# A planner that counts slack behind copies, sums and low parts, and a second phase with fewer low parts on VectorE

## The chip, the core and the metric

The kernel runs on one core of a Trainium2 chip. The metric is device time in microseconds of one execution. The time before is the median of three runs, 1119.76 us (1118.62 to 1120.52). Instructions run on five engines, each in its own program order: PE (TensorE, the matrix products; PEld is its weight load), DVE (VectorE), ACT (ScalarE), POOL (GpSimd) and SP (SyncE, which issues most DMAs). They wait for each other by semaphores alone. An instruction that waits holds up all that stands behind it on its engine.

## The reference

Block-causal attention over 8 x 8 heads of 576 x 64, and behind it a feed-forward layer on 4608 tokens:

```python
scores = scale * np.matmul(q, k.transpose(0, 1, 3, 2))
scores = np.where(block_i >= block_j, scores, -1000000000.0)
attn = softmax(scores)
x = np.matmul(attn, v)          # reshaped to 4608 x 512
h = x @ w_in                    # 512 -> 2048
g = np.maximum(h, 0.0) + alpha * np.minimum(h, 0.0)
out = g @ w_out                 # 2048 -> 512
```

## The kernel before

**Two phases.** The first runs the attention and, beside it, 6 of the 16 blocks of 128 hidden columns. The second, from about 625 us on, runs the other 10, as 5 pairs (`NG`), over 9 blocks of 512 tokens. It computes both layers by a scheme of seven block products instead of eight (Strassen's, in Winograd's form).

**Operands in two parts.** A product of the second phase takes both operands as a high part (rounded to the matmul's type by ACT, line 532) and a low part (the rest: operand minus high part, line 533, on DVE or POOL). Each block product is six matmuls of 128x256: high x high, low x high and high x low, in two halves. I call those six matmuls one product.

**First layer of a pair** (`pair1`, product at line 722). Its seven products are, with the names that the texts below use: A (11·11), B (12·21), C (s2·t2), D (s1·t1), E (s3·t3), F (22·t4), G (s4·22). A, C, E and F add up in one PSUM bank, x. A is written; ACT copies the bank out (`keep`, line 731, u1); C is added onto it; ACT copies it again (u2); E is added; ACT copies it a third time (u3); F is added. So C, E and F must each wait until the copy before them has read x. B goes to bank y, and DVE adds u1 to it (`onto`, line 735). D goes to bank z. DVE then adds z to u3 (line 753), and only then may G be added onto z: **E, copy, DVE sum, G** is the longest chain of a pair. Relu and slope (`act`: line 739 on ACT, line 740 on DVE) make of the banks five tiles c, 128x256.

**Second layer** (`chunk2`, product at line 780). Seven products k = 0 to 6, each over the 5 pairs g, so 35 products a block. Each takes one tile c or a sum of such tiles, split into Gh (ACT, 532) and Gl (533). The low part is on DVE where g is odd (or, in the last block, where g is not 0), else on POOL. Of the sums (`plus`, line 765), three for each g come before k = 2 (`second`: s3, c12 + c22, then c12 - c11, all on DVE) and one before k = 6 (on POOL). `finish` and `onto` (798, 793) add the bank to what the first phase left.

**Beside it**, the seven operands X of the next 512 tokens are made (`factors`): sums at line 549 on DVE, split at 532 and 533, 128x512, three low parts on DVE and four on POOL.

**What sets the order.** A block's first-layer products run beside the second-layer products of the block before. Their order is made by a planner (`Plan.schedule`) when the program is built: it simulates the engines with a modelled cost for each operation (`c_dve`, `c_act`, `c_pool`, `c_mm`, all but PE times `LONGER`) and a latency behind it (`LAT`), and starts whatever is ready with the smallest `prio`. In the second phase a pair's product has `prio` = turn + k (`starts1`), a product of the second layer turn + g (`starts2`), and its split comes `LEAD` = 6 earlier. The modelled times order the instructions and nothing else: on the chip each engine runs them in that order and waits where an input is late.

Of the kernel before, what the change touches and what calls it, by code (L numbers as in the profile page):

```python
# [9 lines left out]
F32 = mybir.dt.float32  # L10
# [19 lines left out]
CHA = 256  # L30
# [107 lines left out]
class Plan:  # L138


    def __init__(self):
        self.ops, self.writer, self.readers = [], {}, {}
        self.free, self.tiles, self.quota, self.last = {}, {}, {}, {}

    def room(self, kind, n, make):
# [6 lines left out]
            have.append(slot)  # L152
        self.quota[kind] = self.quota.get(kind, 0) + n

    def op(self, engine, cost, fn, r=(), w=(), prio=0.0, claim=(), then=None, ends=()):

        i = len(self.ops)
        prio += SHIFTS.get(round(prio, 4), 0.0)
        deps = {j for j, o in enumerate(self.ops) if any(b.kind in ends for b in o[4])} if ends else set()
        for k in r:  # L160
            if k in self.writer:
                deps.add(self.writer[k])
        for k in w:
            if k in self.writer:
                deps.add(self.writer[k])
            deps.update(self.readers.get(k, ()))
        for k in r:
            self.readers.setdefault(k, []).append(i)
        for k in w:
            self.writer[k] = i  # L170
            self.readers[k] = []
        bufs = dict.fromkeys(k[0] if isinstance(k, tuple) else k for k in (*r, *w, *claim))
        bufs = [b for b in bufs if isinstance(b, Buf)]
        for b in bufs:
            b.users += 1
            if b.users == 1 and b.turn:
                b.after = self.last.get(b.turn)
                self.last[b.turn] = b
        deps.discard(i)
        self.ops.append((engine, cost, fn, deps, bufs, prio, then))  # L180
        return i

    def schedule(self):
# [43 lines left out]
        while events:  # L227
# [13 lines left out]
            for engine, heap in ready.items():  # L241
# [135 lines left out]
def attn_ffn(ctx, tc, qT, kT, vT, w_in, w_out, alpha, out):  # L377
# [149 lines left out]
            out=mb(), in0=mb(), scalar=2.0 ** -20, in1=eb(), op0=ALU.mult, op1=ALU.mult), r=[eb], w=[mb], prio=prio)  # L527
        return mb, mb

    def split(src, hi, lo, n, r, hk, lk, claim, on, prio):  # L530

        op("ACT", c_act(n, True), lambda: nc.scalar.copy(out=hi(), in_=src()), r=r, w=[hk], claim=claim, prio=prio)  # L532
        op(on, c_pool(n) if on == "POOL" else c_dve(n), lambda: (nc.gpsimd if on == "POOL" else nc.vector).tensor_tensor(  # L533
            out=lo(), in0=src(), in1=hi().bitcast(F32), op=ALU.subtract), r=[*r, hk], w=[lk], claim=claim, prio=prio)

    wts = {}

# [8 lines left out]

    def add(e, n, to, a, b, f, prio, r=()):

        op(e, c_pool(n) if e == "POOL" else c_dve(n), lambda: (nc.gpsimd if e == "POOL" else nc.vector).tensor_tensor(  # L549
            out=to[1](), in0=a[1](), in1=b[1](), op=f), r=[a[0], b[0], *r], w=[to[0]], prio=prio)  # L550

    w1s = {}
# [156 lines left out]
    def pair1(f, X, turn):  # L709

        W = w1s[f]
        ps = [Buf("bank", "hp", "hp") for _ in range(3)]
        cs = [Buf("c") for _ in range(5)]

        def product(bank, a, x, k, first):
            at, B = W1AT[a], X[x]

            def mm():
                n = 0
                for i, j in ((0, 0), (1, 0), (0, 1)):  # L720
                    for c in range(2):
                        nc.tensor.matmul(bank()[:, :CHA], W()[:, i, 256 * at + P * c:256 * at + P * c + P], B()[:, j, CHA * c:CHA * c + CHA],  # L722
                                         start=(first and n == 0), stop=(n == 5), skip_group_check=True)
                        n += 1
            op("PE", 6 * c_mm(CHA), mm, claim=[W, *(cs if k == 0 else ())],
               r=[(("w1", f, at // 2 * 2), "h"), (("w1", f, at // 2 * 2), "l"), (B, "h"), (B, "l")], w=[bank], prio=turn + k)

        def keep(bank):

            u = Buf("g")  # L730
            op("ACT", c_act(CHA), lambda: nc.scalar.copy(out=u(), in_=bank()[:, :CHA]), r=[bank], w=[u], prio=FP)
            return u

        def onto(bank, u):
            op("DVE", c_dve(CHA), lambda: nc.vector.tensor_tensor(out=bank()[:, :CHA], in0=bank()[:, :CHA], in1=u(), op=ALU.add), r=[u], w=[bank], prio=FP)  # L735

        def act(f, src, v, c):
            g = Buf("g")
            op("ACT", c_act(CHA), lambda: nc.scalar.activation(out=g(), in_=v(), func=AF.Relu, scale=-1.0), r=[src], w=[g], prio=FP)
            op("DVE", c_dve(CHA) + 60, lambda: nc.vector.scalar_tensor_tensor(  # L740
                out=c(), in0=g(), scalar=oal[:, f:f + 1], in1=v(), op0=ALU.mult, op1=ALU.add), r=[src, g, "oal"], w=[c], prio=FP)
        x, y, z = ps
        product(x, "11", "11", 0, True)
        u1 = keep(x)
        product(y, "12", "21", 1, True)
        onto(y, u1)
        act(f, y, lambda: y()[:, :CHA], cs[0])
        product(x, "s2", "t2", 2, False)
        u2 = keep(x)
        product(z, "s1", "t1", 3, True)  # L750
        product(x, "s3", "t3", 4, False)
        u3 = keep(x)
        op("DVE", c_dve(CHA), lambda: nc.vector.tensor_tensor(out=u3(), in0=z()[:, :CHA], in1=u3(), op=ALU.add), r=[z], w=[u3], prio=FP)  # L753
        act(f + 1, u3, u3, cs[3])
        product(x, "22", "t4", 5, False)
        act(f + 1, x, lambda: x()[:, :CHA], cs[2])
        product(z, "s4", "22", 6, False)
        onto(z, u2)
        act(f, z, lambda: z()[:, :CHA], cs[1])
        return cs  # L760

    def chunk2(t0, cs, turn, last):

        def plus(to, a, b, f, on, prio):
            op(on, c_pool(CHA) if on == "POOL" else c_dve(CHA), lambda: (nc.gpsimd if on == "POOL" else nc.vector).tensor_tensor(  # L765
                out=to(), in0=a(), in1=b(), op=f), r=[a, b], w=[to], prio=prio)

        def product(k, bank, c, at, first):

            for g in range(NG):  # L770
# [1 line left out]
                gh, gl, W, v = Buf("Gh"), Buf("Gl"), Buf("w2"), c(g, t - LEAD)  # L772
                op("SP", 256, lambda g=g, W=W: nc.sync.dma_start(out=W().bitcast(F32), in_=wd[at, :, g]),
                   r=[("wd", 1, at, g, x) for x in range(2)], w=[W], prio=t - AHEAD2)
                split(v, gh, gl, CHA, [v], gh, gl, [], "DVE" if g % 2 or last and g else "POOL", t - LEAD)

                def mm(g=g, gh=gh, gl=gl, W=W):
                    for i in range(2):
# [34 lines left out]
        def second(g, prio):  # L813

            c11, c12, _, c22, s3 = cs[g]
            plus(s3, c11, c12, ALU.subtract, "DVE", prio)
            plus(c12, c12, c22, ALU.add, "DVE", prio)
            plus(c11, c12, c11, ALU.subtract, "DVE", prio)
            return c11
        x, y, z = (Buf("bank", "acc") for _ in range(3))  # L820
        o11, o12, o22, o21 = (quarter(i, j) for i, j in ((0, 0), (0, 1), (1, 1), (1, 0)))
# [9 lines left out]
        finish(o22, z, 1, 1)  # L831
        product(5, x, lambda g, prio: cs[g][3], 4, False)
        finish(o21, x, 1, 0)
        product(6, z, sums(2, 2, 0, ALU.subtract, "POOL"), 3, False)
        finish(o12, z, 0, 1, 2 if last else 1)

    def chunk_a(t0, parts=(0, 1)):
# [433 lines left out]
```

## Time and profile before

| | |
|---|---|
| time, median of 3 runs | 1119.76 us (1118.62 to 1120.52) |
| the profiled execution, its own time | 1117.95 us |
| its span, first to last instruction | 1115.8 us |
| granted TensorE clock | 0.998 |
| PE, DVE, ACT, POOL busy | 96%, 73%, 63%, 60% |
| first matmul of `pair1` | 625.3 us |
| last matmul of `chunk2` | 1112.0 us |
| PE's waits in the second phase, 625 us to the end | 27.2 us in 30 waits |

The span is that of the profiled execution; what lies around it, 2.1 us, is launch and end. PE is the engine to look at: its idle time is what can go without fewer or shorter matmuls. A group row of the profile reads: line, engine, operation, tiles out<-in, shape, count | busy us, mean ns of one | idle time just before, and who ended it. A row of the timeline reads: start us, duration us, engine, line, operation, tiles, count, and in brackets the idle time before it with its releaser.

### The profile page before, as it was taken

The numbers are of one execution on the slowest core, as the hardware profiler recorded it, in microseconds if no ns is written. First come the engines' busy times: TensorE is split into PE (matmuls) and PEld (weight loads), VectorE is DVE, ScalarE is ACT, GpSimd is POOL, SyncE is SP. The second block draws the span as 40 slices with busy tenths as digits, with TensorE's granted clock in tenths as the row PEclk, the third lists the DMA queues.
The fourth block names the chain that finished last, engine by engine and source line by source line (L and its number), as shares of the span: only waits on it lengthen the run. The fifth ranks groups of instructions, "written<-read, shape, count | busy, mean of one in ns | idle before, by whom it ended". The sixth has DMA issues, their size and how long they took to land.

```text
span 1115.8 us, 24537 instructions
## 1 busy us (share of the span) xinstructions
PE 1073.9 (96%) x8158; PEld 969.9 (87%) x8158; DVE 814.1 (73%) x1779; ACT 701.4 (63%) x1969; POOL 666.2 (60%) x837
## 2 busy tenths in 40 slices
PE   7999999999999999999999989999999999999998
PEld 4668888888888888898888889999989898989998
DVE  8886685676575745757558598879696969787776
ACT  7788877776666766758555564555455555545554
POOL 4767757667676666666489574636272736364522
PEclk9999999999999999999999999999999999999999
DMA  6687886876668795749044436767676868686875
GB/s 193 194 257 214 233 246 169 267 209 194 193 176 248 217 270 157 214 140 271 32 175 152 174 119 199 243 212 243 211 253 202 276 193 280 188 267 196 270 259 162
DMA packets 139486, 233.37 MB, mean 209 GB/s; under 512 B 14816, under 2 KB 51680, under 8 KB 139360
## 3 DMA queue, kind: packets, MB, share of 16 engines
q1 hardware_dynamic: 138928, 231.53, 68.0%
q8 instruction: 65, 1.06, 0.4%
q14 instruction: 61, 0.50, 0.1%
q10 hardware_dynamic: 432, 0.27, 0.1%
HBM read 150.22 MB, written 37.49 MB: 168 GB/s over the span
## 4 chain that ended last, share of the span: by engine, by line
PE 85%; DVE 9%; ACT 2%; issue 2%; DMA 1%; POOL 1%; DVEq 0%; ACTq 0%; POOLq 0%
PE bank L780 17%; PE bank L722 16%; PE bank L646 13%; PE bank L679 13%; PE bank L1120 8%; PE bank L979 6%; PE bank L1019 6%; PE bank L1049 2%; DVE X L533 2%; DVE c L765 2%; PE bank L1076 1%; DVE xt L549 1%; DVE bank L735 1%; PE bank L984 1%; DVE gl L533 1%
## 5 line engine op out<-in xcount | busy, mean ns | idle before, releaser
L722 PE MATMUL bank<-X,w 128*128 128x256 f32 x1890 | 251.7, 284 | 23.0 <-DVE g L753 13.0
L722 PEld LDWEIGHTS bank<-X,w 128*128 128x128 f32 x1890 | 235.2, 189 | 28.8 <-DVE g L753 15.2
L780 PE MATMUL bank<-w,gh 128*128 128x256 f32 x1260 | 228.9, 280 | 0.8 <-ACT gh L532 0.8
L1011 POOL TENSOR_SCALAR p<-p,ri 128x256 f32<-128x256 f32 (+3 forms) x256 | 141.3, 567 | 90.9 <-DVE ri L1009 42.5
L780 PEld LDWEIGHTS bank<-w,gh 128*128 128x128 f32 x1260 | 193.6, 189 | 1.0 <-ACT gh L532 1.0
L780 PE MATMUL bank<-w,gl 128*128 128x256 f32 x630 | 177.6, 282 | 3.5 <-DVE gl L533 3.5
L533 POOL TENSOR_TENSOR gl<-c,gh 128x256 fp32r<-128x256 f32 x112 | 95.2, 855 | 121.4 <-ACT gh L532 120.3
L1003 ACT ACTIVATE p<-bank,nm 128x256 f32<-128x256 f32 (+3 forms) x256 | 133.9, 532 | 28.2 <-DVE nm L1000 13.8
L679 PE MATMUL bank<-wa,gh 128*128 128x512 f32 x432 | 140.1, 405 | 0.0
L646 PE MATMUL bank<-xh,wa 128*128 128x256 f32 x864 | 128.0, 287 | 0.0
L780 PEld LDWEIGHTS bank<-w,gl 128*128 128x128 f32 x630 | 118.9, 189 | 4.7 <-DVE gl L533 4.7
L532 ACT CAST gh<-c 128x256 fp32r<-128x256 f32 x198 | 79.7, 407 | 62.6 <-PE bank L780 60.6
L646 PEld LDWEIGHTS bank<-xh,wa 128*128 128x128 f32 x864 | 113.6, 190 | 2.7 <-issue 0.9
L1019 PE MATMUL bank<-ident,p 128*128 128x128 f32 x640 | 100.2, 277 | 5.0 <-POOL p L1011 2.9
L666 POOL TENSOR_TENSOR gl<-g,gh 128x256 fp32r<-128x256 f32 x108 | 83.2, 773 | 32.4 <-ACT gh L663 26.7
L1000 DVE TENSOR_REDUCE nm<-bank 128x1 f32<-128x384 f32 (+3 forms) x144 | 80.4, 587 | 22.5 <-PE bank L979 18.8
L979 PE MATMUL bank<-K,Q 128*128 128x512 f32 (+1 forms) x448 | 94.5, 331 | 1.1 <-ACT pl L1063 0.9
L1120 PE MATMUL bank<-PTF,vraw 128*64 128x320 f32 (+3 forms) x768 | 94.1, 384 | 0.5 <-ACT PTF L1096 0.5
L1019 PEld LDWEIGHTS bank<-ident,p 128*128 128x128 f32 x640 | 76.0, 142 | 16.8 <-POOL p L1011 6.6
L659 DVE SCALAR_TENSOR_TENSOR g<-g,oal,bank 128x256 f32<-128x256 f32 x108 | 51.4, 476 | 48.3 <-ACT g L657 47.9
L679 PEld LDWEIGHTS bank<-wa,gh 128*128 128x128 f32 x432 | 75.6, 189 | 12.4 <-issue 0.5
L679 PE MATMUL bank<-wa,gl 128*128 128x512 f32 x216 | 85.8, 397 | 0.1
(162 smaller groups left out, 2210.4 us busy)
## 6 DMA issues: line engine op xcount, KB each, us to landing
w<-wd SPq DMA_DIRECT2D x315, 256.0 KB, 4.0
Q<-QH SPq DMA_DIRECT2D x56, 256.0 KB, 3.9
K<-KH SPq DMA_DIRECT2D x112, 128.0 KB, 3.8
vraw<-in_v SPq DMA_DIRECT2D x32, 320.0 KB, 3.7
qraw<-in_q SPq DMA_DIRECT2D x30, 320.0 KB, 4.0
xd<-xT SPq DMA_DIRECT2D x8, 1152.0 KB, 6.5
part<-o SPq DMA_DIRECT2D x36, 256.0 KB, 3.5
xb<-xd SPq DMA_DIRECT2D x9, 1024.0 KB, 7.9
```

What stands on the lines that cost most here:

```text
L533: op(on, c_pool(n) if on == "POOL" else c_dve(n), lambda: (nc.gpsimd if on == "POOL" else nc.vector).tensor_tensor(out=lo(), in0=src(), in ...
L646: nc.tensor.matmul(hp()[:, :n], ww()[:, 0, cc * P:(cc + 1) * P], x()[:, cc, :n], start=(i == 0 and cc == 0), stop=(i == 2 and cc == NCC - 1))
L666: op("POOL", c_pool(CHA), lambda: nc.gpsimd.tensor_tensor(out=gl(), in0=g(), in1=gh().bitcast(F32), op=ALU.subtract), r=[g, gh], w=[gl], p ...
L679: nc.tensor.matmul(acc(), a()[:, ts], ww(), start=(first and i == 0), stop=(last and i == 2))
L722: nc.tensor.matmul(bank()[:, :CHA], W()[:, i, 256 * at + P * c:256 * at + P * c + P], B()[:, j, CHA * c:CHA * c + CHA], start=(first and n ...
L780: nc.tensor.matmul(bank()[:, CHA * i:CHA * i + CHA], a()[:, P * i:P * i + P], W()[:, x], start=(first and g + i + n == 0), stop=(g == NG - ...
L979: nc.tensor.matmul(o, Q()[:, i, qs], K()[:, 2 * h + i, :w], start=(i == 0), stop=(i == 1))
L1000: op("DVE", c_dve(w), lambda h=h: nc.vector.tensor_reduce(out=nm()[:, h:h + 1], in_=sb[h]()[:, off[h]:off[h] + w], axis=AX.X, op=ALU.max, ...
L1003: op("ACT", 238 + w / 1.2, lambda h=h, t=t: nc.scalar.activation(out=t()[:, :w], in_=sb[h]()[:, off[h]:off[h] + w], func=AF.Exp, bias=nm() ...
L1011: op("POOL", 244 + w / 1.2, lambda h=h: nc.gpsimd.tensor_scalar(out=pts[h]()[:, :w], in0=pts[h]()[:, :w], scalar1=ri()[:, h:h + 1], scalar ...
L1019: nc.tensor.transpose(out=tp()[:, base + c * P:base + (c + 1) * P], in_=pts[h]()[:, c * P:(c + 1) * P], identity=ident)
L1120: nc.tensor.matmul(ob()[rows[h], a - q0:q1 - q0], V()[:, c, h, :], moving, start=(c == 0), stop=(c == cs[-1][0]))
```

## The change

Four edits, all of them on the second phase:

- `SLACK`: 300 ns are added to the modelled latency behind `keep`'s copies, the sum of line 753 and the low parts of `chunk2`. `c_ss` (65 + 1.5 n ns) replaces `c_dve` (65 + n/0.96) as the modelled cost of DVE sums and low parts that read two tiles of SBUF. Both act on the planner alone.
- `LO_DVE = (1,)`: of the low parts of a block only that of g = 1 stays on DVE, and that of g = 3 goes to POOL (the last block keeps g = 1 to 4 on DVE).
- `SUMS`: of the three sums before k = 2, c12 + c22 and c12 - c11 go from DVE to POOL, and the sum before k = 6 goes from POOL to DVE.
- F and G get turn + 6 and + 7 instead of + 5 and + 6.

```diff
+SSN, SLACK = 1.5, 300
+SUMS, LO_DVE = ("DVE", "POOL", "POOL", "DVE"), (1,)
...
-                lat = LAT.get(engine, 0)
+                lat = LAT.get(engine, 0) + self.slack[chosen]
...
+def c_ss(n):
+    return SS(65 + n * SSN)
...
-    def split(src, hi, lo, n, r, hk, lk, claim, on, prio):
+    def split(src, hi, lo, n, r, hk, lk, claim, on, prio, slack=0):
...
-        op(on, c_pool(n) if on == "POOL" else c_dve(n), lambda: (nc.gpsimd if on == "POOL" else nc.vector).tensor_tensor(
-            out=lo(), in0=src(), in1=hi().bitcast(F32), op=ALU.subtract), r=[*r, hk], w=[lk], claim=claim, prio=prio)
+        op(on, c_pool(n) if on == "POOL" else c_ss(n), lambda: (nc.gpsimd if on == "POOL" else nc.vector).tensor_tensor(
+            out=lo(), in0=src(), in1=hi().bitcast(F32), op=ALU.subtract), r=[*r, hk], w=[lk], claim=claim, prio=prio, slack=slack)
...
-            op("ACT", c_act(CHA), lambda: nc.scalar.copy(out=u(), in_=bank()[:, :CHA]), r=[bank], w=[u], prio=FP)
+            op("ACT", c_act(CHA), lambda: nc.scalar.copy(out=u(), in_=bank()[:, :CHA]), r=[bank], w=[u], prio=FP, slack=SLACK)
...
-        product(x, "22", "t4", 5, False)
+        product(x, "22", "t4", 6, False)
         act(f + 1, x, lambda: x()[:, :CHA], cs[2])
-        product(z, "s4", "22", 6, False)
+        product(z, "s4", "22", 7, False)
...
-                split(v, gh, gl, CHA, [v], gh, gl, [], "DVE" if g % 2 or last and g else "POOL", t - LEAD)
+                split(v, gh, gl, CHA, [v], gh, gl, [], "DVE" if g in LO_DVE or last and g else "POOL", t - LEAD, SLACK)
...
-            plus(s3, c11, c12, ALU.subtract, "DVE", prio)
-            plus(c12, c12, c22, ALU.add, "DVE", prio)
-            plus(c11, c12, c11, ALU.subtract, "DVE", prio)
+            plus(s3, c11, c12, ALU.subtract, SUMS[0], prio)
+            plus(c12, c12, c22, ALU.add, SUMS[1], prio)
+            plus(c11, c12, c11, ALU.subtract, SUMS[2], prio)
...
-        product(6, z, sums(2, 2, 0, ALU.subtract, "POOL"), 3, False)
+        product(6, z, sums(2, 2, 0, ALU.subtract, SUMS[3]), 3, False)
```

`c_ss` also replaces `c_dve` in `add` and `plus`. The changed file has 11 lines more ahead of these places: 532, 533, 549, 722, 731, 735, 740, 753, 765 and 780 before are 543, 544, 560, 733, 742, 746, 751, 764, 776 and 791 after. The texts below use the numbers of before throughout.

Three places where the order changes:

**PE, the fourth pair of the 512 tokens 1536 to 2047.** Line 722 is a product of the pair, line 780 one of the second layer, four rows for its six matmuls. Before, from E (X0) over one product of the second layer to F (X6) and G (X1):

```order
L722 MATMUL bank1_180<-X0_6724,w14_7275 128x256 x6
L780 MATMUL bank4_207<-w25_7245,gh5_1120 128x256 x2
L780 MATMUL bank4_207<-w25_7245,gl5_1138 128x256
L780 MATMUL bank4_207<-w25_7245,gh5_1120 128x256 x2
L780 MATMUL bank4_207<-w25_7245,gl5_1138 128x256
L722 MATMUL bank1_180<-X6_7252,w14_7275 128x256 x6
L722 MATMUL bank0_178<-X1_6733,w14_7275 128x256 x6
```

Now, from E (X1) to F (X6) and G (X2):

```order
L733 MATMUL bank7_145<-X1_6732,w14_7277 128x256 x6
L791 MATMUL bank1_180<-w27_7252,gh1_610 128x256 x2
L791 MATMUL bank1_180<-w27_7252,gl1_631 128x256
L791 MATMUL bank1_180<-w27_7252,gh1_610 128x256 x2
L791 MATMUL bank1_180<-w27_7252,gl1_631 128x256
L791 MATMUL bank1_180<-w28_7257,gh2_680 128x256 x2
L791 MATMUL bank1_180<-w28_7257,gl2_698 128x256
L791 MATMUL bank1_180<-w28_7257,gh2_680 128x256 x2
L791 MATMUL bank1_180<-w28_7257,gl2_698 128x256
L733 MATMUL bank7_145<-X6_7254,w14_7277 128x256 x6
L733 MATMUL bank3_186<-X2_6753,w14_7277 128x256 x6
```

Two products instead of one now stand between E and F. In every pair but a block's first, D also goes ahead of C now, which puts two products (B and D) between A and C instead of one. Over a steady block, with "." for a product of the second layer and a bar behind each k, the PE order from k = 0 on was `.....|ABCD.E.FG...|.....|ABCD.E.FG...|ABCD.E.FG...|ABCDE.FG....|ABCD.E..FG..|`, and is now `G....A.|BCD.E..F.G.|.....|ABDC..E..FG.|ABDC..E..FG.|ABDC..E..FG.|ABDC..E..F.|`; the last G of a block now stands behind the bar.

**DVE, the fifth pair of the same tokens**, from `onto` (735) to the sum of line 753 that G waits for. Before:

```order
L735 TENSOR_TENSOR bank6_223<-bank6_223,g6_6804 128x256
L765 TENSOR_TENSOR raw1_176<-c10_7431,raw1_176 128x256
L533 TENSOR_TENSOR X5_7247<-xt1_6726,X5_7247 128x512
L740 SCALAR_TENSOR_TENSOR c17_7546<-g0_481,oal_83,bank6_223 128x256
L549 TENSOR_TENSOR xt1_6726<-xb0_6610,xt1_6726 128x512
L533 TENSOR_TENSOR X4_7241<-xt0_6712,X4_7241 128x512
L753 TENSOR_TENSOR g4_6761<-bank7_145,g4_6761 128x256
```

Now (735 is 746, 765 is 776, 533 is 544, 753 is 764):

```order
L746 TENSOR_TENSOR bank4_207<-bank4_207,g6_6792 128x256
L544 TENSOR_TENSOR X5_7250<-xt1_6734,X5_7250 128x512
L751 SCALAR_TENSOR_TENSOR c17_7543<-g5_6774,oal_83,bank4_207 128x256
L560 TENSOR_TENSOR xt1_6734<-xb0_6610,xt1_6734 128x512
L544 TENSOR_TENSOR X7_7471<-xt0_6712,X7_7471 128x512
L544 TENSOR_TENSOR gl4_951<-c2_7322,gh4_944 128x256
L764 TENSOR_TENSOR g0_481<-bank6_223,g0_481 128x256
```

The sum (765) has left this stretch and a low part (gl4) has come into it.

**POOL, from the middle of that pair to the first pair of the next tokens**, now:

```order
L776 TENSOR_TENSOR raw0_158<-raw0_158 128x256
L544 TENSOR_TENSOR X1_6732<-xb0_6610,X1_6732 128x512
L544 TENSOR_TENSOR gl5_1138<-c0_7226,gh5_1120 128x256
L544 TENSOR_TENSOR gl0_506<-raw1_176,gh0_495 128x256
L544 TENSOR_TENSOR X6_7254<-xt1_6734,X6_7254 128x512
L544 TENSOR_TENSOR gl1_631<-c17_7543,gh1_610 128x256
L544 TENSOR_TENSOR gl2_698<-c11_7507,gh2_680 128x256
L544 TENSOR_TENSOR gl4_951<-c6_7409,gh4_944 128x256
L544 TENSOR_TENSOR gl5_1138<-c8_7379,gh5_1120 128x256
L544 TENSOR_TENSOR gl0_506<-c4_7331,gh0_495 128x256
L544 TENSOR_TENSOR gl1_631<-raw1_176,gh1_610 128x256
L776 TENSOR_TENSOR c2_7322<-raw0_158,c2_7322 128x256
```

and ACT at the end of that stretch, where it rounds this c2 (543), between two copies of bank x of the next pair (742):

```order
L750 ACTIVATE g5_6774<-bank1_180 128x256
L742 COPY g0_481<-bank7_145 128x256
L543 CAST gh2_680<-c2_7322 128x256
L742 COPY g2_665<-bank7_145 128x256
L543 CAST gh3_824<-c0_7226 128x256
```

Ahead of these POOL rows stand X3, X0 and one more sum, behind them three more sums. The sum c2 was on DVE before; in its place POOL had sums for k = 6, whose results nothing needed soon. On ACT the copy u3 (g2, the second 742) stands behind the rounding of c2, as it did before.

More of the change, by code (lines that the diff above doesn't have):

```diff
@@ L141, in __init__ @@
     def __init__(self):
-        self.ops, self.writer, self.readers = [], {}, {}
+        self.ops, self.writer, self.readers, self.slack = [], {}, {}, []
         self.free, self.tiles, self.quota, self.last = {}, {}, {}, {}
@@ L153, in room, with op @@
         self.quota[kind] = self.quota.get(kind, 0) + n
-    def op(self, engine, cost, fn, r=(), w=(), prio=0.0, claim=(), then=None, ends=()):
+    def op(self, engine, cost, fn, r=(), w=(), prio=0.0, claim=(), then=None, ends=(), slack=0):
         i = len(self.ops)
@@ L180, in op @@
         self.ops.append((engine, cost, fn, deps, bufs, prio, then))
+        self.slack.append(slack)
         return i
@@ L321, in c_dve @@
     return 65 + n / 0.96
+class SS(float):
+    pass
+def c_ss(n):
+    return SS(65 + n * SSN)
 def c_dve2(n):
@@ L547, in add @@
     def add(e, n, to, a, b, f, prio, r=()):
-        op(e, c_pool(n) if e == "POOL" else c_dve(n), lambda: (nc.gpsimd if e == "POOL" else nc.vector).tensor_tensor(
+        op(e, c_pool(n) if e == "POOL" else c_ss(n), lambda: (nc.gpsimd if e == "POOL" else nc.vector).tensor_tensor(
             out=to[1](), in0=a[1](), in1=b[1](), op=f), r=[a[0], b[0], *r], w=[to[0]], prio=prio)
@@ L752, in pair1 @@
         u3 = keep(x)
-        op("DVE", c_dve(CHA), lambda: nc.vector.tensor_tensor(out=u3(), in0=z()[:, :CHA], in1=u3(), op=ALU.add), r=[z], w=[u3], prio=FP)
+        op("DVE", c_dve(CHA), lambda: nc.vector.tensor_tensor(out=u3(), in0=z()[:, :CHA], in1=u3(), op=ALU.add), r=[z], w=[u3], prio=FP, slack=SLACK)
         act(f + 1, u3, u3, cs[3])
-        product(x, "22", "t4", 5, False)
+        product(x, "22", "t4", 6, False)
         act(f + 1, x, lambda: x()[:, :CHA], cs[2])
-        product(z, "s4", "22", 6, False)
+        product(z, "s4", "22", 7, False)
         onto(z, u2)
@@ L764, in plus @@
         def plus(to, a, b, f, on, prio):
-            op(on, c_pool(CHA) if on == "POOL" else c_dve(CHA), lambda: (nc.gpsimd if on == "POOL" else nc.vector).tensor_tensor(
+            op(on, c_pool(CHA) if on == "POOL" else c_ss(CHA), lambda: (nc.gpsimd if on == "POOL" else nc.vector).tensor_tensor(
                 out=to(), in0=a(), in1=b(), op=f), r=[a, b], w=[to], prio=prio)
```

## The prediction

> **What bounds the kernel now.** The page first: PE is busy for nearly the whole span.
>
> ```profile
> PE 1073.9 (96%) x8158; PEld 969.9 (87%) x8158; DVE 814.1 (73%) x1779; ACT 701.4 (63%) x1969; POOL 666.2 (60%) x837
> ```
>
> The change leaves every matmul as it is, so it can win only idle time of PE. The view of waits of PE says where that lies. First 713.5 to 1034.8 us, six steady blocks of 53.55 us; then 625 to 713.5 (the run-in); then 1034.8 to the end.
>
> ```profile
> PE bank L722 <- DVE g L753: 7.7, 6, 1.3
> PE bank L722 <- ACT g L731: 5.0, 6, 0.9
> PE bank L780 <- DVE gl L533: 3.5, 6, 0.6
> ...
> PE bank L722 <- DVE g L753: 5.3, 5, 1.5
> PE bank L722 <- ACT g L731: 3.1, 4, 1.5
> PE bank L722 <- ACT X L532: 1.0, 1, 1.0
> ...
> PE bank L722 <- ACT g L731: 0.9, 1, 0.9
> PE bank L780 <- ACT gh L532: 0.8, 1, 0.8
> ```
>
> Each steady block has the same three waits, six times over: 1.28 us at G of its fifth pair, 0.83 at E of its first, 0.58 in a product of the second layer. The windows of one steady block and of the last block with pairs, which has one wait alone, bear that out:
>
> ```profile
> 767.10:820.70 53.60, 50.84 (x423) 50.18 (x422) 43.75 (x79) 28.94 (x77) 27.10 (x31) 1.00 0.73 231
> 1034.80:1086.00 51.20, 50.34 (x422) 50.10 (x421) 37.99 (x75) 26.61 (x72) 20.45 (x26) 1.00 0.83 273
> ```
>
> Columns are length, then busy us of PE, PEld, DVE, ACT, POOL. The timeline says why G waits:
>
> ```profile
> 812.39 0.43 DVE L735 TENSOR_TENSOR bank<-bank,g 128x256 f32<-128x256 f32 x1 [0.20 <-PE bank L722]
> 812.63 1.30 POOL L533 TENSOR_TENSOR X<-xb,X 128x512 fp32r<-128x512 f32 x1 [0.43 <-ACT X L532]
> 812.73 1.48 DVE L765 TENSOR_TENSOR raw<-c,raw 128x256 f32<-128x256 f32 x1
> 814.14 0.68 DVE L533 TENSOR_TENSOR X<-xt,X 128x512 fp32r<-128x512 f32 x1
> 814.33 0.88 PE L722 MATMUL bank<-X,w 128*128 128x256 f32 x6
> ...
> 815.04 0.40 PE L780 MATMUL bank<-w,gh 128*128 128x256 f32 x2
> 815.13 1.39 DVE L549 TENSOR_TENSOR xt<-xb,xt 128x512 f32<-128x512 f32 x1
> 816.21 1.45 POOL L533 TENSOR_TENSOR X<-xb,X 128x512 fp32r<-128x512 f32 x1 [0.24 <-ACT X L532]
> 816.44 1.77 DVE L533 TENSOR_TENSOR X<-xt,X 128x512 fp32r<-128x512 f32 x1
> 816.44 0.87 PE L722 MATMUL bank<-X,w 128*128 128x256 f32 x6
> 818.13 0.41 DVE L753 TENSOR_TENSOR g<-bank,g 128x256 f32<-128x256 f32 x1
> 818.60 0.97 PE L722 MATMUL bank<-X,w 128*128 128x256 f32 x6 [1.28 <-DVE g L753]
> ```
>
> DVE runs without a gap from line 735 to line 753, and the sum that G needs is last in its queue. A product takes 0.71 us (814.33 to 815.04). F to G took 2.16 instead, and G's own six matmuls 0.97 instead of 0.87: this wait costs 2.16 - 0.71 + 0.10 = 1.55 us, **0.26 more than its idle time**. So a steady block loses 0.83 + 0.58 + 1.28 + 3 x 0.26 = 3.5 us, and one without waits would take 53.55 - 3.5 = 50.1. The last block agrees: 51.2 less 0.9 + 0.26 is 50.0.
>
> Why E waits:
>
> ```profile
> 824.65 0.85 DVE L765 TENSOR_TENSOR c<-c,raw 128x256 f32<-128x256 f32 x1
> 825.42 0.95 DVE L533 TENSOR_TENSOR gl<-c,gh 128x256 fp32r<-128x256 f32 x1
> 826.30 0.95 DVE L765 TENSOR_TENSOR c<-c,c 128x256 f32<-128x256 f32 x1
> 827.18 0.68 DVE L793 TENSOR_TENSOR m<-bank,m 128x512 f32<-128x512 f32 x1
> 827.78 0.42 DVE L735 TENSOR_TENSOR bank<-bank,g 128x256 f32<-128x256 f32 x1
> 828.23 0.39 ACT L739 ACTIVATE g<-bank 128x256 f32<-128x256 f32 x1 [2.54 <-DVE bank L735]
> 828.51 0.37 ACT L731 COPY g<-bank 128x256 f32<-128x256 f32 x1
> ```
>
> The copy u2 (731) was ready long before, but on ACT it stands behind a Relu (739) that waits for line 735, and that stands on DVE behind two sums and a low part. The third wait is a low part on DVE, `gl` of g = 3, issued 0.88 us before PE needs it:
>
> ```profile
> 836.24 0.82 DVE L533 TENSOR_TENSOR gl<-raw,gh 128x256 fp32r<-128x256 f32 x1
> 837.12 0.38 PE L780 MATMUL bank<-w,gl 128*128 128x256 f32 x1 [0.59 <-DVE gl L533]
> ```
>
> **The change part by part.** Prices of what moves, from the groups of 713.5 to 1034.8 us, and two rows of the timeline in which the other engine does not disturb:
>
> ```profile
> L533 DVE TENSOR_TENSOR gl<-c,gh 128x256 fp32r<-128x256 f32 x49 | 30.3, 619 | 10.1 <-ACT gh L532 9.7
> L765 DVE TENSOR_TENSOR c<-c,c 128x256 f32<-128x256 f32 x25 | 18.4, 735 | 0.2
> L533 POOL TENSOR_TENSOR gl<-c,gh 128x256 fp32r<-128x256 f32 x80 | 68.2, 859 | 76.3 <-ACT gh L532 75.4
> L533 POOL TENSOR_TENSOR X<-xb,X 128x512 fp32r<-128x512 f32 x18 | 27.0, 1501 | 5.8 <-ACT X L532 5.8
> L765 POOL TENSOR_TENSOR c<-c,c 128x256 f32<-128x256 f32 x15 | 11.8, 792 | 3.4 <-DVE gl L533 3.4
> ...
> 824.20 0.41 DVE L765 TENSOR_TENSOR o<-c,c 128x256 f32<-128x256 f32 x1
> 827.83 0.72 POOL L765 TENSOR_TENSOR c<-c,raw 128x256 f32<-128x256 f32 x1
> ```
>
> *Loads.* A block moves 7 low parts (g = 3 of seven k) and 10 sums from DVE to POOL, and 5 sums back. DVE loses 7 x 0.62 + 5 x 0.74 = 8.0 of 43.8 us a block; POOL gains 7 x 0.86 + 5 x 0.79 = 10.0 on top of 27.1. In a block of some 51 us DVE comes to 70% and POOL to 73%. Neither becomes the bound by its sum; what counts is where they are late.
>
> *The low part at 837.12.* Low parts of g = 3 are now on POOL, and `LEAD` puts this one six products ahead of its use on an engine that idles before such rows (75.4 us behind ACT in POOL's row). The wait goes: **-0.84** a block. On DVE the next candidate is the low part of g = 1 for k = 3, behind three X operations, 793 and 735: they sum to about what the nine products ahead of it leave. I take 0 for it, and 0.3 as the other end.
>
> *E of the first pair.* In the new DVE order one sum stands ahead of 793 and 735 where two sums and a low part stood, because c12 + c22 and c12 - c11 are on POOL. 735 then runs at the end of B, two products before the copy u2 is needed. **-1.09**; at worst half of it stays.
>
> *G of the fifth pair.* From the end of B to G stood seven products, 5.0 us, against 5.7 us of DVE (812.39 to 818.13) and the sum itself. Now stand nine, 6.4 us. On DVE the 1.48 of a sum is gone and a low part (0.41 to 0.95) has come: 5.7 - 1.48 + 0.62 = 4.9 us, and with 0.41 for the sum and some 0.3 of signals 5.6. That fits with 0.8 us to spare, so **-1.54**; if all its operations with two inputs in SBUF are as slow as the 1.77, 0.4 remains.
>
> *The other pairs* had no wait with one product between E and F; they have two now, which costs nothing, since the second layer's products only change place.
>
> *A new wait.* ACT rounds c2 (the first operand of k = 2) between the copies u2 and u3 of the next first pair, and c2 now comes from POOL. Between A of the fifth pair and that sum POOL has four X low parts, eight low parts and three sums: by their means 4 x 1.50 + 8 x 0.86 + 3 x 0.79 = 15.3 us, or 21.5 products. F stands 25 products behind that A; POOL's first X low part can start some 2.5 behind A, and the rounding of c2 must begin 1.5 before F, which leaves 21. So POOL is late by some 0.4 us, and with 0.26 for the wait itself F pays about **+0.6**. Bounds: 0, if they run as alone (0.72 for 0.79); and 2.5, if POOL and DVE never overlap, since DVE has some 4 us of such work in the stretch, half of which the means hold already.
>
> Against that stands a rule of the Trainium skill ("SBUF — State Buffer", Who interferes with whom): a VectorE instruction with two SBUF inputs contends with a GpSimd instruction that reads SBUF, one blocking the other for its whole length. The rows agree: DVE's 1.77 at 816.44 is 1.09 over its 0.68 and ends 0.55 behind POOL's 1.45, while line 753, with one input in PSUM, keeps its 0.41. A low part alone takes 0.41 on DVE and 0.72 on POOL, so by that rule each move raises the demand on what they share, and the new wait would lie at its upper end.
>
> *Sum.* Six steady blocks: 6 x (-0.84 - 1.09 - 1.54 + 0.6 + 0.4) = -14.8, the 0.4 for the two ends above that are close to nothing to spare. The last block's wait at E: -1.1. The run-in has 9.4 us in 10 waits, 12.0 us by the price above; with two products between most E and F (one before), but little of the second layer to put there, I take a quarter: -3, between 0 and -8. The 0.8 at the end and the first phase stay; its order differs only in its last tens of us (±1). Together **-19**: 1117.95 - 19 = 1099 for the profiled execution. That lay 1.8 below the median of the runs, so I expect **1101**.
>
> **The rivals.** *The new wait is large* (POOL 2 to 3 us late in each block): 2.5 instead of 0.6 and the 0.4 at 0.8 give -5 to -8, so 1112 to 1115. For it: POOL has no idle time in that stretch. Against: before, POOL had as many X low parts there and idled between them. *One wait stays*: line 753 is as late as now, because DVE's operations grow longer as POOL fills up, and the run-in gains nothing: 6 x (-0.84 - 1.09 + 0.6) - 1.1 = -9, so 1111. For it: 1.48, 1.39 and 1.77 stand beside POOL's X low parts, and those stay. *Slower:* POOL and DVE share so strictly that c2 is over 3.5 us late. Alone, POOL's operations up to c2 are 13.1 us (0.72 each, X 1.30) and DVE's about 5.5 up to line 753; end to end 18.6 us against 15.0 of 21 products gives 3.6 at F, and low parts of k = 2 queued behind the three next sums add up to 2. It decides from 3.5 us a block; at 5.6 it is 6 x 2.1, less 4 for the last block and the run-in, +9: 1129. For it: POOL's X low part at 816.21 and DVE's at 816.44 ended after 2.00 us together, as long as alone in turn (1.30 + 0.68). Against it: POOL's 1501 and 859 ns, taken beside a DVE with more of such work than it has now, are only 0.2 and 0.14 us above what they take alone, so most of the time the two don't meet. *Nothing changes* would need the new wait to equal the three that go.
>
> **How the numbers follow.** Forecast with its ends 0.62 (1092 to 1108); one wait stays, or POOL is late, 0.22 (1108 to 1117); no change 0.07; slower 0.09. Two runs of this kernel can be told apart from 0.2%, 2.2 us. The range from all waits gone (-30: 1090) to the large new wait (1115) leaves 2 in 10 out. Faster 0.84, same 0.07, slower 0.09.
>
> **What would show it.** In the profile after: no wait on line 753 over 0.5 us in the steady blocks, none on a low part of DVE, the block at 50.5 to 51.5 us; a row of PE <- ACT g L731 at F of the first pair, behind ACT <- POOL c; POOL's low parts over 0.86 us on average, DVE's sums longer than 0.74. Wrong if POOL's sums hold up ACT or DVE for over 2 us in each block, or if the waits only change their name.

## The result, and the profile after

| | before | after |
|---|---|---|
| time, median | 1119.76 us (1118.62 to 1120.52) | 1094.92 us (1093.83 to 1095.69) |
| ratio, 95% interval | | 0.978 [0.976, 0.980] |
| the profiled execution, its own time | 1117.95 us | 1094.51 us |
| its span | 1115.8 us | 1092.7 us |

The change is 24.8 us faster; 1101 was forecast, between 1090 and 1115. Lines of the changed kernel stand in its rows with their own numbers, 11 higher than those that the text uses; 764 is the sum of line 753. Three single executions of later versions took far longer than the others (2667 us of engines_alone, 3624 of no_cost, 1175 of only_low_part_moves) and are left out of the times below.

Engines of the changed kernel, from its page: us busy, share of the span, instructions.

```profile
span 1092.7 us, 24546 instructions
PE 1070.1 (98%) x8158; PEld 966.8 (88%) x8158; DVE 762.5 (70%) x1678; ACT 703.5 (64%) x1969; POOL 746.5 (68%) x938
```

PE has the same 8158 matmuls, busy 3.8 us less, in a span that is 23.1 us shorter: 19.3 us of it is idle time of PE, and the 3.8 are for the most part matmuls that took longer behind a wait, as the prediction put it. Its waits in the changed kernel, first over the six steady blocks (707.0 to 1011.4 us), then over the run-in (625 to 707 us); columns are total us, times, longest:

```profile
PE bank L733 <- DVE g L764: 2.1, 6, 0.4
...
PE bank L733 <- ACT g L742: 1.2, 2, 0.6
PE bank L791 <- POOL gl L544: 1.1, 2, 0.6
PE bank L733 <- DVE X L544: 1.0, 1, 1.0
PE bank L733 <- POOL X L544: 0.8, 3, 0.3
PE bank L791 <- DVE gl L544: 0.4, 1, 0.4
```

The three waits of a steady block (7.7, 5.0 and 3.5 us in all) are gone, and one has come, 0.31 to 0.38 us in each. The run-in's 9.4 us in 10 waits are 4.5 in 9; five behind the sum of line 753, the largest group, are gone entirely. Windows of the run-in, of one steady block and of the last block with pairs (length, busy us of PE, PEld, DVE, ACT, POOL, then the granted clock):

```profile
625.00:707.00 82.00, 77.55 (x624) 74.75 (x623) 62.43 (x109) 49.70 (x132) 64.54 (x66) 1.00 0.63 199
...
808.50:859.30 50.80, 50.42 (x422) 49.93 (x421) 37.50 (x67) 29.25 (x77) 36.68 (x43) 1.00 0.77 244
1011.40:1062.90 51.50, 51.15 (x428) 50.72 (x427) 33.23 (x65) 27.25 (x73) 33.87 (x43) 1.00 0.85 282
```

A steady block takes 50.7 us (304.4 over six; before 53.55). DVE falls from 43.75 to 37.5 us and POOL rises from 27.1 to 36.7; the two come to 74% and 72% of the block. So the time came from here: run-in -6.3, six steady blocks -16.9, last block +0.3, start of the second phase -0.2, the tail behind the last pairs unchanged (26.0 us): -23.1, the span's difference. A steady block's last G now stands behind its end, so the run-in hands on one product (0.71 us) and the last block receives it: like for like these two are -5.6 and -0.4.

The one wait that came, from the timeline of the changed kernel (start us, duration, engine, line, operation, tiles, count, idle before it and its releaser):

```profile
816.80 0.97 PE L733 MATMUL bank<-X,w 128*128 128x256 f32 x6
...
817.07 1.45 POOL L776 TENSOR_TENSOR c<-raw,c 128x256 f32<-128x256 f32 x2
...
817.86 0.41 ACT L543 CAST gh<-c 128x256 fp32r<-128x256 f32 x1 [1.12 <-POOL c L776]
817.86 0.94 DVE L776 TENSOR_TENSOR c<-c,c 128x256 f32<-128x256 f32 x1 [0.87 <-POOL c L776]
...
818.17 0.37 ACT L742 COPY g<-bank 128x256 f32<-128x256 f32 x1
...
818.73 0.96 DVE L544 TENSOR_TENSOR gl<-c,gh 128x256 fp32r<-128x256 f32 x1
...
819.02 0.86 PE L733 MATMUL bank<-X,w 128*128 128x256 f32 x6
...
819.61 0.95 DVE L776 TENSOR_TENSOR c<-c,c 128x256 f32<-128x256 f32 x1
...
820.49 0.41 DVE L764 TENSOR_TENSOR g<-bank,g 128x256 f32<-128x256 f32 x1
...
820.96 0.98 PE L733 MATMUL bank<-X,w 128*128 128x256 f32 x6 [0.38 <-DVE g L764]
```

The cause is the foreseen one: POOL's two sums of 817.07 are late, and ACT waits 1.12 us to round the first of them, c2, ahead of the copy u3 (742). But F (819.02) still finds u3 in time. What is late is the queue on DVE: the same lateness holds a sum for k = 6 for 0.87 us, and that sum, a low part and a second sum, 0.95 us each beside POOL, stand ahead of line 753 (820.49). G waits for that.

Prices of what moved, from the groups of the six steady blocks of the changed kernel (count | busy us, mean ns | idle time ahead, releaser):

```profile
L544 POOL TENSOR_TENSOR gl<-c,gh 128x256 fp32r<-128x256 f32 x98 | 81.4, 841 | 45.2 <-ACT gh L543 43.5 <-PE bank L791 1.6
...
L776 POOL TENSOR_TENSOR c<-c,c 128x256 f32<-128x256 f32 x26 | 22.2, 858 | 6.2 <-DVE c L776 3.7 <-DVE raw L776 2.6
...
L544 DVE TENSOR_TENSOR gl<-c,gh 128x256 fp32r<-128x256 f32 x30 | 20.3, 675 | 8.9 <-ACT gh L543 8.9
...
L776 DVE TENSOR_TENSOR c<-c,c 128x256 f32<-128x256 f32 x22 | 15.8, 719 | 4.5 <-POOL c L776 2.6 <-POOL gl L544 1.9
```

Beside their rows before (859, 792, 619 and 735 ns), none of these four has changed by more than a tenth, though POOL does 9.6 us more of such work in each block. Two larger operations that stayed on DVE grew by more: the low part X<-xb from 677 to 901 ns, the sum xt<-xb,xt from 1034 to 1210. So DVE's load fell by 6.3 us a block, where the prediction reckoned with 8.0. The cause shows in the steady blocks before: DVE's 75 sums and low parts of 128x256 during which POOL was idle took 0.41 to 0.43 us each, the 48 with POOL busy all along 0.96 on average.

### The profile page after: what moved, and what is told of

Its sections match the earlier page's. It is cut to its first block, busy times and chain, and to the rows that moved or that the text cites. A ratio compares the mean times of both kernels' runs of the same rounds, so it can differ in the third digit from the quotient of the medians.

```text
span 1092.7 us, 24546 instructions
## 1 busy us (share of the span) xinstructions
PE 1070.1 (98%) x8158; PEld 966.8 (88%) x8158; DVE 762.5 (70%) x1678; ACT 703.5 (64%) x1969; POOL 746.5 (68%) x938
## 4 chain that ended last, share of the span: by engine, by line
PE 86%; DVE 6%; POOL 3%; ACT 2%; issue 2%; DMA 1%; ACTq 0%; DVEq 0%; POOLq 0%
PE bank L791 18%; PE bank L733 17%; PE bank L657 13%; PE bank L690 13%; PE bank L1131 8%; PE bank L1030 6%; PE bank L990 6%; PE bank L1060 2%; PE bank L1087 1%; POOL gl L544 1%; PE bank L995 1%; DVE gl L544 1%; DVE c L776 1%; POOL w L544 1%; POOL gl L677 1%
## 5 line engine op out<-in xcount | busy, mean ns | idle before, releaser
L544 POOL TENSOR_TENSOR gl<-c,gh 128x256 fp32r<-128x256 f32 x137 | 113.6, 839 | 70.0 <-ACT gh L543 68.4
L670 DVE SCALAR_TENSOR_TENSOR g<-g,oal,bank 128x256 f32<-128x256 f32 x108 | 51.4, 477 | 50.5 <-ACT g L668 50.1
```

The source lines that it names most:

```text
L544: op(on, c_pool(n) if on == "POOL" else c_ss(n), lambda: (nc.gpsimd if on == "POOL" else nc.vector).tensor_tensor(out=lo(), in0=src(), in1 ...
```

## The experiments

The change has three parts that do something: the slack behind copies, sums and low parts; the higher modelled cost; and the moves between engines. The fourth does nothing: with turns 5 and 6 or 6 and 7 for F and G, every engine's program is the same, on top of the kernel before and on top of the change. So the later place of F comes from the slack: with it two products stand between E and F of every pair in the steady blocks (slack_alone, no_cost), without it one, but for the fifth pair (cost_alone, engines_alone, no_slack). Two theories, named in the expectations: *distance* (the waits go because the new order leaves time behind what is waited for; the moves matter little) and *load* (they go because DVE has less to do ahead of it; the order matters little).

Every diff below is against the changed kernel, and the turns are left out of them. Ratios are to the kernel before on the same chip (medians 1119.1, 1119.1 and 1118.8 us in the three groups of four). All in one table; "block" is the mean of six steady blocks, "run-in" the time from 625.0 us to their start, both of the profiled execution. Six of the twelve times lie outside every range that their expectation names (cost_alone, no_cost, old_order_new_engines, k6_sums_on_pool, only_low_part_moves, k6_sums_later), five of them above: neither theory foretold how the parts add up.

| label | kept of the change | time, us | ratio [95%] | run-in | block |
|---|---|---|---|---|---|
| (before) | nothing | 1119.8 | 1 | 88.5 | 53.55 |
| slack_alone | slack | 1118.1 | 0.999 [0.998, 1.000] | 87.5 | 53.9 |
| cost_alone | cost | 1126.1 | 1.007 [1.004, 1.009] | 91.8 | 54.35 |
| engines_alone | moves | 1111.2 | 0.993 [0.991, 0.995] | 88.5 | 52.3 |
| slack_and_cost | slack, cost | 1117.4 | 0.998 [0.997, 1.000] | 89.1 | 52.9 |
| no_slack | cost, moves | 1103.8 | 0.986 [0.985, 0.988] | 87.2 | 51.45 |
| no_cost | slack, moves | 1100.6 | 0.983 [0.981, 0.985] | 87.4 | 51.3 |
| (the change) | all | 1094.9 | 0.978 [0.976, 0.980] | 82.0 | 50.7 |

**slack_alone**

```diff
-    return SS(65 + n * SSN)
+    return c_dve(n)
-SUMS, LO_DVE = ("DVE", "POOL", "POOL", "DVE"), (1,)
+SUMS, LO_DVE = ("DVE", "DVE", "DVE", "POOL"), (1, 3)
```

> The kernel before with the 300 ns of slack alone (old cost of sums and low parts, old engines). Its order has two products between E and F and D ahead of C in every pair. Theory 'distance' (the waits go because more products stand between a bank's copy or sum and its next product): the waits at E and G of the steady blocks go or fall under 0.5 us, that on VectorE's low part of g = 3 may stay (0.6); steady block 50.5 to 51.5 us, time 1098 to 1106. Theory 'load' (the waits go because VectorE has fewer operations with two SBUF inputs): VectorE keeps 43 to 44 us of work in each block, and at least two of the three waits stay; block over 52.5, time 1110 to 1120.

PE's waits in its six steady blocks:

```profile
PE bank L733 <- DVE g L764: 15.5, 6, 2.6
PE bank L733 <- ACT g L742: 0.6, 2, 0.3
```

Three waits (2.7 us a block) have become one, at G of the fifth pair, of 2.58 us. The slack does spread each pair's chain, and the low part no longer waits and E hardly; but DVE has as much to do as before, and line 753 now comes 7.6 us behind line 735 (810.21 to 817.84) where it came 5.7 behind. Distance without relief moves the wait and does not end it. PE's clock takes back a part of what the slack does win (last section).

**cost_alone**

```diff
-SSN, SLACK = 1.5, 300
-SUMS, LO_DVE = ("DVE", "POOL", "POOL", "DVE"), (1,)
+SSN, SLACK = 1.5, 0
+SUMS, LO_DVE = ("DVE", "DVE", "DVE", "POOL"), (1, 3)
```

> The kernel before with the new modelled cost of VectorE's sums and low parts alone (no slack, old engines). Its PE order in the steady blocks is that of before, one product between E and F; only VectorE's own queue changes order. Distance: the same three waits or nearly, 1112 to 1121. Load: the same, since no operation changes engine, 1115 to 1121. A rival to both, that the order within VectorE's queue is what matters: waits at G shorter by more than half, 1105 to 1111.

```profile
PE bank L733 <- ACT g L742: 8.0, 6, 1.4
PE bank L733 <- DVE g L764: 7.7, 6, 1.3
PE bank L791 <- DVE gl L544: 5.4, 6, 0.9
```

These are its waits over the same blocks: the three places of before, two of them longer. The truer cost alone loses 7 us. Modelled, a 128x256 sum on DVE was (65 + 256/0.96) x 1.12 = 371 ns (`LONGER` is 1.12) and is (65 + 1.5 x 256) x 1.12 = 503, where the trace of before has 735 on average: nearer, but nearer is not yet a better order.

**engines_alone**

```diff
-SSN, SLACK = 1.5, 300
+SSN, SLACK = 1.5, 0
-    return SS(65 + n * SSN)
+    return c_dve(n)
```

> The kernel before with the moves between VectorE and GpSimd alone (low part of g = 3, three sums; no slack, old cost). PE order of the steady blocks as before, one product between E and F. Load: the waits at E and on VectorE's low part go, that at G of the fifth pair falls under 0.7 us; block 51 us, time 1098 to 1104. Distance: the low part's wait goes with its engine (5 us in all), those at E and G stay at over half their length; time 1108 to 1115.

```profile
PE bank L733 <- DVE g L764: 8.8, 12, 0.8
PE bank L733 <- ACT g L742: 1.2, 1, 1.2
```

Its waits there: those at E and at the low part are gone (one at E in six blocks), G of the fifth pair waits 0.75 instead of 1.28, and G of the first pair now waits too, 0.71. The moves alone bring 8 us, about a third; the run-in gains nothing, with waits of 3.3 and 1.5 us in it and PE at half clock for 6.8 us behind the first (652.4 to 659.2).

**slack_and_cost**

```diff
-SUMS, LO_DVE = ("DVE", "POOL", "POOL", "DVE"), (1,)
+SUMS, LO_DVE = ("DVE", "DVE", "DVE", "POOL"), (1, 3)
```

> The kernel before with slack and the new cost, old engines. Two products between E and F. Distance: no steady wait over 0.5 us, time 1095 to 1102, close to the whole change. Load: over 1108, since VectorE's 43 us a block stay.

```profile
PE bank L733 <- ACT g L742: 10.4, 6, 1.8
PE bank L791 <- DVE gl L544: 4.4, 6, 0.8
```

Now G of the fifth pair no longer waits, but E of the first pair waits 1.73 where it waited 0.83, and the low part 0.73. With all of the new planning and the old loads the gain is 2 us: distance by itself is refuted. Load by itself is too: *engines_alone*, *no_slack* and *old_order_new_engines* have the loads of the change, and took 1111.2, 1103.8 and 1125.6 us.

**no_slack** and **no_cost** (each takes one part away from the full change)

```diff
-SSN, SLACK = 1.5, 300
+SSN, SLACK = 1.5, 0
```

> The change without the 300 ns of slack (new cost and new engines). Its PE order in the steady blocks is nearly that of before, one product between E and F. Distance: waits at G (and E) of over 0.5 us in each block, time 1104 to 1113. Load: as the change, 1093 to 1099.

```diff
-    return SS(65 + n * SSN)
+    return c_dve(n)
```

> The change without the new modelled cost (slack and new engines). Two products between E and F, but no product of the second layer more ahead of a block's last G. Distance: 1093 to 1099. Load: 1093 to 1099 too. A rival, that the planner must know how long VectorE's sums are: over 1103.

Waits in the steady blocks, first of no_slack:

```profile
PE bank L733 <- DVE g L764: 4.4, 6, 0.8
```

and of no_cost:

```profile
PE bank L733 <- DVE g L764: 4.0, 6, 0.7
PE bank L733 <- ACT g L742: 2.5, 6, 0.4
```

Both keep G of the fifth pair (0.74 and 0.66 us), no_cost has 0.42 at E of the second pair besides, and both have nearly the whole run-in of before (87.2 and 87.4, against 82.0 of the change, 0.7 of it for the product that it hands on). The slack is worth 9 us with the moves in place (1103.8 to 1094.9) and the cost 6, where alone they were worth 1 and -7. Each needs the others.

**old_order_new_engines** and **new_order_old_engines.** These two separate the order from the load. The planner plans with one set of engines (`on`), and the instruction is issued on another (`run`), so that every engine's rows keep the planned place; lines are 3 higher again than in the changed kernel.

```diff
+RUN = ("DVE", "POOL", "POOL", "DVE")
...
-    def split(src, hi, lo, n, r, hk, lk, claim, on, prio, slack=0):
+    def split(src, hi, lo, n, r, hk, lk, claim, on, prio, slack=0, run=None):
...
-            plus(s3, c11, c12, ALU.subtract, SUMS[0], prio)
+            plus(s3, c11, c12, ALU.subtract, SUMS[0], prio, RUN[0])
```

The first has slack 0, the old cost, `SUMS` and `LO_DVE` of before, and runs on the new engines; the second is planned as the change is and runs on the engines of before.

> The order of the kernel before on every engine, instruction for instruction, but the low parts of g = 3 and the sums run where the change puts them (each takes the place in its new engine's queue that its turn in the plan gives). Load: the waits at E and on the low part go, G under 0.7 us, time 1100 to 1106. Distance: at most half of the 27 us of waits goes, 1108 to 1116.

> The order of the change, but the low parts of g = 3 and the sums run where they ran before. Distance: most of the gain stays, 1096 to 1103; VectorE's 43 us a block may bring back part of the wait at G of the fifth pair. Load: the three waits come back at over half their length, 1106 to 1116.

Waits in the steady blocks, first of old_order_new_engines:

```profile
PE bank L794 <- POOL gl L547: 8.5, 11, 1.2
PE bank L736 <- DVE g L767: 7.9, 8, 1.2
```

It took 1125.6 us, 1.006 [1.004, 1.008], block 54.0: slower than before: in an order that did not reckon with them POOL's low parts are late, one or two in each block, and G of the first pair waits 0.65 to 1.21 in five of the six. And of new_order_old_engines:

```profile
PE bank L736 <- DVE g L767: 7.0, 6, 1.2
PE bank L736 <- ACT g L745: 2.9, 6, 0.5
```

It took 1107.1 us, 0.990 [0.988, 0.991], block 51.9. An order made for a lighter DVE gains 12 us even with DVE's old load, more than the order made for that load (slack_and_cost); of the three places, G of the fifth pair keeps 1.16 and E 0.48. The last 12 us need the moves themselves.

**k6_sums_on_pool** (the change's order, but the sums for k = 6 run on POOL again) asks whether the remaining wait at G is DVE's queue.

```diff
+RUN = ("DVE", "POOL", "POOL", "POOL")
```

> The order of the change on every engine, but the five sums before k = 6 run on GpSimd, each at the place that its turn in the plan gives. The change's one steady wait (0.35 us at G of the first pair) stands behind the sum of line 753, and ahead of that on VectorE stand two of these sums, which wait for GpSimd. Theory 'queue': without them the wait goes, 7 x 0.6 us = 4 us, time 1089 to 1092. Rival 'GpSimd is late': the wait is GpSimd's, whose load rises from 36.6 to some 41 us of a block; G's wait stays or a low part on GpSimd becomes late, time 1094 to 1104.

```profile
PE bank L794 <- POOL gl L547: 3.6, 12, 0.8
PE bank L794 <- ACT gh L546: 3.6, 6, 0.8
PE bank L794 <- DVE gl L547: 1.2, 2, 0.6
```

In its steady blocks G of the first pair no longer waits: those two sums ahead of line 753 are the cause of that wait. But the time is 1112.3, 0.995 [0.993, 0.996]: with 40.2 us of work in one block of 52.4, POOL delivers low parts and c sums too late, and products of the second layer wait 1.4 us a block instead. So in this order the move of the k = 6 sums to DVE is worth 17 us; an order planned for them on POOL was not run.

**only_low_part_moves** and **only_sums_move** split the moves.

```diff
-SUMS, LO_DVE = ("DVE", "POOL", "POOL", "DVE"), (1,)
+SUMS, LO_DVE = ("DVE", "DVE", "DVE", "POOL"), (1,)
```

> The change without the moves of sums (slack, new cost, low part of g = 3 on GpSimd). With slack and cost alone a block waited 1.7 us at E of the first pair and 0.75 on a low part of VectorE. If the low part's wait goes with its engine and E's belongs to the sums ahead of line 735, the first goes and the second stays at 1.2 to 1.8: time 1107 to 1112. If any VectorE work taken away helps, both fall: 1100 to 1105.

```diff
-SUMS, LO_DVE = ("DVE", "POOL", "POOL", "DVE"), (1,)
+SUMS, LO_DVE = ("DVE", "POOL", "POOL", "DVE"), (1, 3)
```

> The change without the move of the low part (slack, new cost, the three sums moved). E's wait goes, a low part of VectorE is late by 0.5 to 0.8 us in each block: time 1099 to 1104. If the sums are nothing and only the low part counts: over 1108.

Waits in the steady blocks, of only_low_part_moves, then of only_sums_move:

```profile
PE bank L733 <- ACT g L742: 13.4, 6, 2.3
```

```profile
PE bank L733 <- DVE g L764: 5.3, 6, 0.9
```

The low part without the sums brings nothing: 1118.2 us, 0.999 [0.998, 1.000]; its own wait goes, and E of the first pair waits 2.2 instead, behind the sums that stayed on DVE. PE waits 2.2 us a block where it waited 2.7, and still the block takes 53.7 us: PE's clock falls behind most of these waits (last section). The sums alone bring 1101.7, 0.986 [0.984, 0.987], block 51.4: no wait of E, of the fifth G or of a low part in a steady block, but G of the first pair waits 0.88. So the sums are the greater part, and the low part of g = 3 is worth the last 7 us (some 4 in the blocks, some 2.5 in the run-in, which is 84.5 there).

**k6_sums_later** tries to take the last wait away: the sums for k = 6 also wait until line 793 of k = 2 is done, so that they come behind line 753.

```diff
-                out=to(), in0=a(), in1=b(), op=f), r=[a, b], w=[to], prio=prio)
+                out=to(), in0=a(), in1=b(), op=f), r=[a, b, *after], w=[to], prio=prio)
...
-                plus(cs[g][to], cs[g][a], cs[g][b], f, on, prio)
+                plus(cs[g][to], cs[g][a], cs[g][b], f, on, prio, [o12])
```

> The change, with the sums before k = 6 made to depend on the addition behind k = 2 (line 793), so that the planner cannot put them ahead of the first pair's sum of line 753. Two pairs of the block now overlap in PE's order. Queue: the wait at G of the first pair goes: 1089 to 1093. Rival: the sums crowd behind k = 2, where VectorE holds the X operations, and another wait of 0.5 us or more comes: 1095 to 1100.

```profile
PE bank L791 <- DVE gl L544: 9.7, 6, 1.7
```

In its steady blocks the wait at G is gone, and a low part on DVE in a later k is 1.6 us late: 1103.8, 0.987 [0.986, 0.988]. A wait of 0.35 us was exchanged for one of 1.6. No version that was run beats the change.

## Why the prediction was right, point by point

The profiled execution is 23.4 us shorter where 19 were forecast. Of the 4.4 between them the steady blocks hold 2.1 and the run-in 2.6; the last block falls short by 0.7, and 0.5 lie ahead of the second phase and around the span.

- **What bounds it.** Right: the same matmuls, and the span fell by 23.1 us with PE's idle time and the slow products behind it. The price of a wait as idle time plus 0.26 holds: before, waits cost 3.5 us a block; now 0.35 + 0.26 = 0.6; the difference, 2.9, is 17.2 over six blocks, and 16.9 was measured.
- **The three waits that go** (-0.84, -1.09, -1.54). Right, each in full; the allowance of 0.4 for what had little to spare wasn't needed. Over six blocks it is 2.4 us, which accounts for the 2.1 by which the blocks came out better than the -14.8. What the prediction did not see is how the three hang together. It told each as a local matter of which instructions stand ahead. The runs show that a part of the change ends one or two of the waits and lengthens another or brings a new one: 2.58 at G (slack_alone), 1.73 at E (slack_and_cost), 2.2 at E (only_low_part_moves), 0.71 at G of the first pair (engines_alone). The cost alone ends none.
- **The new wait** (+0.6, between 0 and 2.5, at F). The price was right, 0.35 + 0.26. Its origin was right: c2's sum on POOL late, ACT's rounding waiting for it. Its place was off by one step: F still came in time, and G waits, through DVE's queue. k6_sums_on_pool shows that by taking the two sums out of that queue.
- **Durations.** "POOL's low parts over 0.86 us on average, DVE's sums longer than 0.74" was wrong: 841 and 719 ns. POOL's sums (858 ns, from 792) and DVE's low parts (675, from 619) grew instead, by 8 and 9%, and two of DVE's 128x512 operations by 33 and 17%, so that DVE's load fell by 6.3 us a block and not by 8.0. By the rule of the Trainium skill that the prediction weighed ("SBUF — State Buffer", Who interferes with whom) the new wait would have lain at its upper end, 2.5; the three DVE rows of 0.94 to 0.96 us beside POOL, against 0.41 alone, show the contention that it states, but the wait came to 0.35 of idle time. One reason shows in the same rows: side by side DVE starts such an operation every 0.88 us (817.86 to 820.49), and so does POOL, which is less than the 1.13 that the two take alone in turn (0.41 and 0.72), so neither is held up for the other's whole length. Another is likely, but no run separates it: DVE and POOL, idle for a quarter of a block, paid for some of the contention out of that time.
- **The last block** (-1.1). Mis-sized: -0.4 like for like. Its one wait at E is gone, and 0.3 at G of its first pair has come, which the prediction had counted for the steady blocks alone.
- **The run-in** (-3, 0 to -8). Mis-sized: -5.6. A quarter of its waits was taken where nearly half went, those of line 753 all of them. The runs with one part missing have 87.2 (no_slack), 87.4 (no_cost) and 84.5 (only_sums_move) of 88.5, so this, too, takes the parts together. Which order there does it was not taken apart further.

*Slower* and *the new wait is large* fell with the wait of 0.35; *one wait stays* did not come true for the change, but it is what no_slack and no_cost show, with 0.74 and 0.66 at that very place and 1103.8 and 1100.6 us.

## What to carry to other kernels

An order made by a planner and the loads that it plans for are one thing: moving work to another engine in an old order lost 6.5 us here, planning better for the old loads won 2, and both together won 25. In these runs a wait that was taken out mostly came back at another place of the same queue, unless that queue got shorter, so ask for each edit which instruction is late next, and judge it together with its companions and not alone. Give what a bottleneck engine waits for a margin in the plan when real durations depend on the neighbour: a 128x256 sum took 0.41 or 0.95 us on DVE, by what POOL did meanwhile.

## What the hardware showed that was not expected

PE often runs at half clock for a while after a wait of a little over 2 us. From the timeline of slack_alone, PE, around the wait of 2.59 us:

```profile
818.30 0.99 PE L733 MATMUL bank<-X,w 128*128 128x256 f32 x6 [2.59 <-DVE g L764]
...
819.73 0.63 PE L791 MATMUL bank<-w,gh 128*128 128x256 f32 x2
820.16 0.41 PE L791 MATMUL bank<-w,gl 128*128 128x256 f32 x1
820.37 0.63 PE L791 MATMUL bank<-w,gh 128*128 128x256 f32 x2
...
822.77 0.41 PE L791 MATMUL bank<-w,gh 128*128 128x256 f32 x2
823.02 0.29 PE L791 MATMUL bank<-w,gl 128*128 128x256 f32 x1
823.14 0.40 PE L791 MATMUL bank<-w,gh 128*128 128x256 f32 x2
```

Three matmuls take 0.64 us (819.73 to 820.37) and later 0.37 (822.77 to 823.14). This lasts from about 819.1 to 822.3 us, five such triples, so 5 x 0.27 = 1.4 us are lost beside the wait. The windows of slack_alone, only_low_part_moves and slack_and_cost over the same stretch show it in the granted clock (the first number behind POOL's):

```profile
819.00:873.00 54.00, 51.43 (x421) 51.23 (x420) 40.98 (x79) 29.68 (x77) 26.41 (x30) 0.97 0.72 230
```

```profile
819.00:873.00 54.00, 51.81 (x423) 51.47 (x423) 39.96 (x72) 29.47 (x79) 32.81 (x38) 0.97 0.73 230
```

```profile
819.00:873.00 54.00, 51.59 (x432) 51.04 (x431) 43.67 (x80) 30.14 (x79) 28.65 (x32) 1.00 0.74 236
```

It is 0.97 with waits of 2.58 and 2.2 us, and 1.00 with one of 1.73. But not every long wait does it. Two more windows of slack_alone run from one wait at G to the next:

```profile
872.40:926.40 54.00, 51.43 (x420) 51.23 (x420) 41.46 (x79) 29.95 (x77) 26.26 (x30) 0.97 0.72 230
926.40:979.50 53.10, 50.22 (x420) 49.82 (x420) 42.60 (x79) 29.48 (x77) 26.57 (x30) 1.00 0.73 233
```

The wait that ends at 926.4 is as long as the others, 2.58 us, and nothing follows it; a block with a slow stretch takes 1.0 us longer than one without. (That is less than the 1.4, for without the stretch E of the next pair waits 0.3 us.) In the trace's record of the clock the slow stretches of slack_alone begin at 764.5, 819.1, 873.8, 979.6 and 1034.2 us and last 3.4 us each. The distances between them are 16, 16, 31 and 16 times 3.41 us, so they lie on one grid. The waits ahead of them have 2.0 us or more within one step of the grid, while that of 926.4 lies across a border (925.0) with 1.1 and 1.4 us on its sides. The other traces agree: from 640 us to 5 us before the end, in all fourteen, each step at full clock with 1.9 us or more of idle time of PE was followed by one at half clock, and none with 1.73 or less was. So what counts in these traces is PE's idle time within one such step; two waits of 1.13 and 0.77 us in one step of old_order_new_engines (986.4 to 989.8) did it too.

So to gather three waits of 1.28, 0.83 and 0.58 us into one of 2.58 is a loss of its own: slack_alone has no less idle time to show for it, and its block is 0.3 us longer, where its blocks without a slow stretch are 0.4 us shorter than before. The run-ins of cost_alone, engines_alone, slack_and_cost, only_low_part_moves, only_sums_move and others hold such stretches too, those of before and of the change none. The Trainium skill ("TensorE: Matmul & The Clock Gate", What's actually happening) states that the clock falls to half after at least one idle window of about 3.4 us; here it fell behind steps of 3.4 us that held 1.9 to 2.9 us of idle time, in an engine that was busy on both sides.
